# One core: attention into two feed-forward layers; attention products per head on 64 rows, a and b side by side in PSUM, the third weight group in one chunk

## The chip, the core and the metric

One core of a Trainium2 chip. The metric is the device time of one execution in microseconds; the kernel before takes 665.56 us (median of three runs). Matrix products run on TensorE (PE; its weight loads are listed as PEld), elementwise work on VectorE (DVE), ScalarE (ACT) and GpSimd (POOL); SyncE (SP) issues all transfers. Matmul results lie in PSUM: eight banks of 512 fp32 columns on 128 partitions.

## The reference

```python
kv = einsum('bhsd,bhse->bhde', k, v)              # 4 sequences, 8 heads, 576 tokens, head width 64
out = einsum('bhsd,bhde->bhse', q, kv)
x = out / sqrt(mean(out * out, -1) + 1e-6) * g_norm   # as 2304 tokens x 512
y = ((x @ w_a) * (x @ w_b)) @ w_out               # 512 -> 1536 -> 512, weights arrive as 64-bit floats
h = y @ w_in                                      # 512 -> 1024
solu = h * softmax(h)
out = layernorm(solu) * g_ln @ w_out2             # 1024 -> 512
```

## The kernel before, in words

All instructions are issued once, in an order that a planner in the kernel writes out: `Order` keeps a clock of its own, every PE item has a cost (`od.pe(cost, ...)`), and every chain of ACT, DVE, POOL and SP steps has due times from such costs. Each engine then runs its instructions in that order and waits only for data.

The 2304 tokens are 18 tiles of 128 (t = 0 to 17). A sequence has 576 tokens, so tiles 4 and 13 belong to two sequences. Two heads make a pair p, four pairs a token.

1. Attention, to about 64 us on PE. `att_kv` (lines 802 to 848) forms k^T v of each head (L822, and the last 64 tokens of a sequence at L830) and copies the two 64 x 64 blocks of a pair onto the diagonal of a 128 x 128 tile of `bds`, whose rest is zero (memset at L312). `att_1` (L850) multiplies q by it: for each pair one fp32 matmul with 128 rows and 128 columns (L868; four a tile, and eight with 64 weight columns in a tile of two sequences). An fp32 matmul stands in the trace as two records, each with its own weight load. A tile's result takes one PSUM bank, one of banks 6 and 7 by turns (`R_PA`), or half a place for tiles 2 and 3 (`EXTRA`). ACT squares it (L905) and copies it out (L907), DVE sums, POOL takes the root, DVE or POOL scales. Tiles 0 to 11 are turned on PE (`att_2`, L961) into ACT L971 and DVE L972; tiles 12 to 17 go through HBM (`att_hop`: `sx`, `yb`, ACT L937 and L941, DVE L942). Either way x ends as a high part `xh` and a low part `xl` in fp32r.

2. First layer, columns in 12 groups f of 128, tokens in six blocks j of 384. Every product of high and low parts is three matmuls (`three`, L978 to L980). For f = 0, 1 (`ab_items`) eight items a block give a = x w_a in one bank of a place (two adjacent banks) and b = x w_b in the other; then ACT copies a to SBUF (L1040), DVE multiplies b by it (L1041) and the product goes to HBM (`store_g`). These items fill PE between attention steps; a block needs its three tiles of x. f = 2, 3 (pair fp = 1) run as `plain_step`, the others (fp = 2 to 5) as `step_items`: a Strassen scheme with seven products per matrix (P1 to P7 in the order of `WSEQ`), for a and b (m = 0, 1) by turns, each accumulator in a bank of its own (`bank_take`), with sums on DVE (L1212, L1261, L1300) and copies on ACT (L1205, L1253, L1262, L1269) for each m apart. `x_sums` (L1056) makes the sums of x for it on DVE (L1078) and ACT (L1082) in banks 4 to 7.

3. Weights are decoded from 64-bit floats (L438 to L459), split into high and low, and stored to HBM in groups (`sums_w`, `to_hbm` through two staging tiles `stg`): for each pair fp and matrix m groups 0 (512 columns), 1 and 2 (sums, only where a Strassen step needs them), 4 and 3 (256 columns each). `w_fill` loads a group into a slot of `wt` when it is free; group 4 shares slot 2 with the weights of f = 1.

4. Then the second product of the first layer (L1382) and the second layer (L1524, the same lines 978 to 980 with `gw`). Nothing in them is changed.

Of the kernel before, what the change touches and what calls it, by code (L numbers as in the profile page):

```python
# [9 lines left out]
F32 = mybir.dt.float32  # L10
# [192 lines left out]
def attention_moe_moe_kernel(ctx: ExitStack, tc, kv_in, kv_tail, q_in, g_norm, w1, w_in, w_out2, g_ln, out):  # L203
# [62 lines left out]
    bds = [M(f"bd{i}", [P, NP, P], F32, M.R2 + 40960 + 2048 * i) for i in range(2)]  # L266
# [21 lines left out]
    a_t = [M(f"a{i}", [P, TB], F32, M.AB + 1536 * i) for i in range(4)]  # L288
    g_t = [M(f"g{i}", [P, TB], F32, (M.AB + 6144, M.AB + 7680, M.R2 + 43008)[i]) for i in range(3)]
    s_t = [[M(f"s{m}{i}", [P, TB], F32, M.R2 + 36864 + 3072 * m + 1536 * i) for i in range(2)] for m in range(2)]  # L290
# [20 lines left out]
    for t in bds:  # L311
        nc.vector.memset(t, 0.0)  # L312
# [94 lines left out]
    STG = Slots(2)  # L407
# [192 lines left out]
    def sums_w(k, f, su, sf, t):  # L600
# [3 lines left out]

        def have(t):
            if i == 0:
                w_pair[fp, m] = f, sf
            else:
                rest(t, *w_pair[fp, m], f, sf)

        def rest(t, w0, s0, w1_, s1):
            h = CH // 2
            extra, summed = has_group(fp, 4), has_group(fp, 1)
            users = {s0: 1 + summed, s1: 1 + extra + summed}
            rank = rank_of(k)
            first = [3]

            def used(s):
                def done(t):
                    users[s] -= 1  # L620
                    if not users[s]:
                        F.give(s)
                        decode_more()
                return done

            def group(g, src, then):
                n = WN[g]

                def fill(hi, lo):
                    return [("A", 0.1 + 0.5 * n / CH, lambda: nc.scalar.copy(out=hi, in_=src)),  # L630
                            ("X", (0.1 + 0.52 * n / CH, 0.2 + 1.12 * n / CH),
                             lambda e: tt(e)(out=lo, in0=src, in1=hi.bitcast(F32), op=ALU.subtract))]

                return lambda t: to_hbm((fp, m, g), n, fill, then, t, rank)
# [4 lines left out]
            def two_sums():  # L639
                a, b = ws_t  # L640

                def part(t):
# [9 lines left out]
                    (None, 0, used(s0)), (None, 0, used(s1)), (None, 0, part),  # L652
                    (None, 0, group(2, b, part)),
                ]

            group(0, w0, used(s0))(t)
            if extra:
                group(4, w1_[:, 0:h], used(s1))(t)

            group(3, w1_[:, h:], used(s1))(t)  # L660
            if not summed:
                return
# [1241 lines left out]
```

## Time and profile before

| | us |
|---|---|
| median of three runs (665.41 to 666.17) | 665.56 |
| the profiled execution | 662.99 |
| its span, first to last instruction | 661.1 |
| PE busy in the span | 647.4 |
| DVE busy | 511.0 |
| ACT busy | 320.9 |
| POOL busy | 217.9 |

The profiled execution is 2.57 us shorter than the median; 1.9 us of it lie outside the span. Times inside rows are from one execution; start times count from the start of the span. "128*64 128x64" is a matmul with 128 rows and 64 columns of weights and 64 moving columns. A row "x16" in a timeline merges 16 instructions; its duration runs to the end of the last one, so the start of the next row tells more of the pace.

### The profile page before, as it was taken

What the parts mean: (1) busy time and instruction counts of PE and PEld (TensorE: products, weight loads), DVE (VectorE), ACT (ScalarE), POOL (GpSimd) and SP (SyncE); (2) the same over time, 40 slices, a digit from 0 to 9 for tenths busy, and PEclk for the clock granted to TensorE, in tenths of its full rate; (3) what the DMA queues carried; (4) which work ended last, traced back from release to release, by engine and by line L of the source; (5) the groups of instructions that cost most, each with busy time, mean ns of one, the idle gap of its engine ahead of it and who ended that gap; (6) DMA issues with size and microseconds to landing.
All of it is one profiled execution on the core that took longest, in us unless ns stands there. A gap on an engine that the chain in (4) does not pass through costs nothing.

```text
span 661.1 us, 10563 instructions
## 1 busy us (share of the span) xinstructions
PE 647.4 (98%) x3674; PEld 594.7 (90%) x3674; DVE 511.0 (77%) x828; ACT 320.9 (49%) x577; POOL 217.9 (33%) x247
## 2 busy tenths in 40 slices
PE   5999999999999999999999999999999999999998
PEld 4899989999999999999999888888888888888887
DVE  2988799988889888998579868786389996677730
ACT  3866552434444434444335445453576665464431
POOL 1777220324221102001023314121677774452100
PEclk9999999999999999999999999999999999999999
DMA  8994787667588796899995644774705464533451
GB/s 329 390 325 159 249 267 256 231 240 285 187 324 313 266 382 251 313 396 373 329 358 164 191 129 128 235 242 154 274 1 175 143 187 148 155 108 105 128 175 49
DMA packets 94486, 150.66 MB, mean 228 GB/s; under 512 B 9568, under 2 KB 61536, under 8 KB 94432
## 3 DMA queue, kind: packets, MB, share of 16 engines
q1 hardware_dynamic: 94432, 149.98, 66.0%
q8 instruction: 29, 0.48, 0.3%
q14 instruction: 25, 0.20, 0.1%
HBM read 93.33 MB, written 56.62 MB: 227 GB/s over the span
## 4 chain that ended last, share of the span: by engine, by line
PE 91%; DMA 3%; DVE 3%; SPq 1%; ACT 1%; issue 1%; POOL 1%; DVEq 0%; ACTq 0%
PE ps L1382 21%; PE ps L979 18%; PE ps L980 18%; PE ps L978 18%; PE ps L1524 13%; PE ps L868 2%; DMA raw<-in_w 1%; DMA kv<-in_kv 1%; DMA yb<-sx 1%; DVE gl L1356 1%; PE ps L961 1%; PE ps L822 1%; SPq L934 1%; POOL r L898 1%; DVE u L455 0%
## 5 line engine op out<-in xcount | busy, mean ns | idle before, releaser
L1382 PE MATMUL ps<-gh,wo 128*128 128x512 f32 (+1 forms) x480 | 137.6, 367 | 0.0
L978 PE MATMUL ps<-xh,wt 128*128 128x384 f32 x384 | 129.6, 338 | 1.0 <-ACT xh L941 1.0
L979 PE MATMUL ps<-xl,wt 128*128 128x384 f32 x384 | 128.4, 334 | 0.3 <-DVE xl L942 0.3
L980 PE MATMUL ps<-xh,wt 128*128 128x384 f32 x384 | 128.3, 334 | 0.0
L1382 PEld LDWEIGHTS ps<-gh,wo 128*128 128x128 f32 x480 | 88.7, 188 | 11.2
L1382 PE MATMUL ps<-gl,wo 128*128 128x512 f32 (+1 forms) x240 | 88.2, 368 | 0.7 <-DVE gl L1356 0.7
L1524 PE MATMUL ps<-bo,ao 128*128 128x512 f32 x378 | 87.3, 389 | 0.0
L1524 PEld LDWEIGHTS ps<-bo,ao 128*128 128x128 f32 x378 | 70.8, 188 | 14.8 <-ACT bt L1565 0.2
L1356 DVE TENSOR_TENSOR gl<-gi,gh 128x512 fp32r<-128x512 f32 (+1 forms) x60 | 48.0, 803 | 35.8 <-ACT gh L1355 35.4
L978 PEld LDWEIGHTS ps<-xh,wt 128*128 128x128 f32 x384 | 72.1, 188 | 1.5 <-ACT xh L941 1.3
L979 PEld LDWEIGHTS ps<-xl,wt 128*128 128x128 f32 x384 | 72.1, 188 | 0.5 <-DVE xl L942 0.5
L980 PEld LDWEIGHTS ps<-xh,wt 128*128 128x128 f32 x384 | 72.1, 188 | 0.0
L1355 ACT CAST gh<-gi 128x512 fp32r<-128x512 f32 (+1 forms) x60 | 34.7, 580 | 76.9 <-PE ps L1382 62.7
L979 PE MATMUL ps<-gw,dh 128*128 128x512 f32 (+1 forms) x152 | 57.4, 378 | 0.0
L980 PE MATMUL ps<-gw,dl 128*128 128x512 f32 (+1 forms) x152 | 57.4, 378 | 0.0
L978 PE MATMUL ps<-gw,dh 128*128 128x512 f32 (+1 forms) x152 | 57.4, 378 | 0.0
L1382 PEld LDWEIGHTS ps<-gl,wo 128*128 128x128 f32 x240 | 45.0, 188 | 6.7 <-DVE gl L1356 1.0
L978 PE MATMUL ps<-th,wt 128*128 128x384 f32 x144 | 48.1, 334 | 0.0
L979 PE MATMUL ps<-tl,wt 128*128 128x384 f32 x144 | 48.1, 334 | 0.0
L980 PE MATMUL ps<-th,wt 128*128 128x384 f32 x144 | 48.1, 334 | 0.0
L438 ACT ACTIVATE u<-raw 128x512 f32<-128x512 f32 x52 | 34.7, 671 | 22.2 <-DMA raw<-in_w 6.4
L450 DVE SCALAR_TENSOR_TENSOR f<-raw,u 128x512 uint32<-128x512 uint32 x52 | 38.8, 745 | 0.4
(136 smaller groups left out, 1214.4 us busy)
## 6 DMA issues: line engine op xcount, KB each, us to landing
raw<-in_w SPq DMA_DIRECT2D x36, 512.0 KB, 5.9
gm<-g SPq DMA_DIRECT2D x72, 192.0 KB, 3.9
hb<-stg SPq DMA_DIRECT2D x26, 512.0 KB, 3.2
wt<-hb SPq DMA_DIRECT2D x26, 512.0 KB, 6.3
gi<-gm SPq DMA_DIRECT2D x36, 256.0 KB, 2.7
su<-ya SPq DMA_DIRECT2D x34, 256.0 KB, 2.5
kv<-in_kv SPq DMA_DIRECT2D x16, 512.0 KB, 7.3
ya<-su SPq DMA_DIRECT2D x32, 256.0 KB, 3.0
```

The costliest lines, as they stand in the source:

```text
L438: nc.scalar.activation(out=u, in_=w[:, :, 1].bitcast(F32), func=AF.Abs)
L450: nc.vector.scalar_tensor_tensor(out=fb, in0=w[:, :, 1], scalar=0xC0000000, in1=ub, op0=ALU.bitwise_and, op1=ALU.bitwise_or)
L822: nc.tensor.matmul(at(p)[h * D:(h + 1) * D], lhsT=k, rhs=v, start=c == 0 and p - pairs[0] < 2, stop=False, skip_group_check=True)
L868: nc.tensor.matmul(ps[m * w:(m + 1) * w, p * P:(p + 1) * P], lhsT=src[:, m * w:(m + 1) * w], rhs=bds[b % 2][:, p], start=True, stop=True)
L898: ("G", 1.76, lambda: nc.gpsimd.tensor_tensor(out=r, in0=r, in1=mhalf[:, 0:H], op=ALU.pow)),
L978: nc.tensor.matmul(o, lhsT=ah, rhs=bh, start=first, stop=False, skip_group_check=skip)
L979: nc.tensor.matmul(o, lhsT=ah, rhs=bl, start=False, stop=False, skip_group_check=skip)
L980: nc.tensor.matmul(o, lhsT=al, rhs=bh, start=False, stop=last, skip_group_check=skip)
L1355: ("A", 0.08 + 0.5 * k, lambda g=g, gh=gh: nc.scalar.copy(out=gh, in_=g)),
L1356: ("S", 0.08 + 0.54 * k, lambda g=g, gh=gh, gl=gl: nc.vector.tensor_tensor(out=gl, in0=g, in1=gh.bitcast(F32), op=ALU.subtract)),
L1382: nc.tensor.matmul(o, lhsT=x, rhs=y, start=f == 0 and n == 0, stop=f == NF1 - 1 and n == 2)
L1524: nc.tensor.matmul(o, lhsT=x, rhs=y, start=first and k == m == 0, stop=k == 1 and m == 2, skip_group_check=not first)
```

## The change

- `bds` holds 64 columns per pair instead of 128: head 0 on partitions 0 to 63, head 1 on 64 to 127. No zeros, no memset.
- `att_1` runs a matmul per head, on 64 rows: eight per tile (weights 64 rows x 128 columns, 64 moving columns), 16 of 64 x 64 in tiles 4 and 13. Head 0 writes one bank, head 1 the next, so a tile takes two banks: 6 and 7 together, or a place if enough are free (`two_banks`, `spare`). `att_2` and single `att_kv` steps take one bank of 6 and 7, or a place. The planner's cost of `att_1` falls from 0.9 (1.2) to 0.5.
- a and b of every block stand in the two banks of a place. In Strassen steps one ACT copy and one DVE sum then serve both m (768 columns instead of 384), the sum V goes to a place of its own, and all blocks end in one function, `product`, which keeps a in the tile that receives the product; the tiles `a_t` go.
- For fp = 1 group 4 has 512 columns and there is no group 3; group 0 is stored as soon as its own chunk is decoded; there is a third staging tile.
- `x_sums` waits until four groups of fp = 1 are in HBM, and ranks behind that pair's decoding.

```diff
-    bds = [M(f"bd{i}", [P, NP, P], F32, M.R2 + 40960 + 2048 * i) for i in range(2)]
+    bds = [M(f"bd{i}", [P, NP, D], F32, M.R2 + 40960 + 1024 * i) for i in range(2)]
...
-    stg = [[M(f"stg{i}{n}", [P, 2, n], F32R, M.STG + 4096 * i) for n in (CH, CH // 2)] for i in range(2)]
+    stg = [[M(f"stg{i}{n}", [P, 2, n], F32R, (M.STG, M.STG + 4096, M.AB)[i]) for n in (CH, CH // 2)]
+           for i in range(3)]
...
-    for t in bds:
-        nc.vector.memset(t, 0.0)
...
+        return plain > 0 if g == 4 else plain < NTB // 2 if g in (1, 2, 3) else True
+
+    def size_of(fp, g):
+        return CH if g == 4 and not has_group(fp, 1) else WN[g]
...
+    own = {6: 0.0, 7: 0.0}
+
+    def spare():
+        return sum(place_time(i) <= od.now for i in range(3)) >= 1 + (od.now > 27)
...
+    def two_banks():
+        if max(own.values()) <= od.now:
+            own[6] = own[7] = INF
+            return PS[:, 6:8], own_done(6, 7)
+        i, ps = ps_tile()
+        return ps, ps_done(i)
...
+    def two_ok():
+        return max(own.values()) <= od.now or spare()
+
+    def one_ok():
+        return min(own.values()) <= od.now or spare()
...
-            if not (R_X.ok() and R_SQ.ok() and R_R.ok()) or INF in ready:
+            if not (R_X.ok() and R_SQ.ok() and R_R.ok() and two_ok()) or INF in ready:
...
-            od.pe(0.9 + 0.3 * (len(seqs(i)) == 2), lambda: att_1(i))
+            od.pe(0.5, lambda: att_1(i))
...
             for m, b in enumerate(bs):
-                nc.tensor.matmul(ps[m * w:(m + 1) * w, p * P:(p + 1) * P], lhsT=src[:, m * w:(m + 1) * w],
-                                 rhs=bds[b % 2][:, p], start=True, stop=True)
+                for h in range(2):
+                    hs = slice(h * D, (h + 1) * D)
+                    nc.tensor.matmul(ps[m * w:(m + 1) * w, h, p * D:(p + 1) * D], lhsT=src[hs, m * w:(m + 1) * w],
+                                     rhs=bds[b % 2][hs, p], start=True, stop=True)
...
+    def product(f, j, slot, ps, t):
+
+        od.chain([(None, 0, when_ok((G_S,), lambda sg: [
+            ("A", AC, lambda: nc.scalar.copy(out=g_t[sg], in_=ps[:, 0, 0:TB])),
+            ("V", VT, lambda: nc.vector.tensor_tensor(out=g_t[sg], in0=ps[:, 1, 0:TB], in1=g_t[sg], op=ALU.mult)),
+            ps_done(slot), store_g(f, j, sg)]))], t=t)
...
-        if not sum_q or att_left[0]:
+        if not sum_q or att_left[0] or sum(k[0] == 1 for k in w_in_hbm) < 4:
...
-        rank = 4.5
+        rank = 5.075
...
-            parts = [[(0, 0), (0, 1)], [(4, 0), (3, 0)]][i]
+            parts = [[(0, 0), (0, 1)], [(4, 0), (3, 0) if mixed else (4, 1)]][i]
...
+            if name == "P1":
+                od.chain([("A", 2 * AC - 0.1, lambda: nc.scalar.copy(out=s1, in_=pair_of(X[1]))), is_("s1")], t=w)
...
+            def add(o, a, b):
+                return ("V", 2 * VT - 0.15, lambda: nc.vector.tensor_tensor(out=o, in0=a, in1=b, op=ALU.add))
+
+            if once("u0", ("P6", "made"), "s1"):
+                y = pair_of(Y[1])
+                od.chain([add(y, y, s1), ("A", 2 * AC - 0.1, lambda: nc.scalar.copy(out=s1, in_=y)),
+                          (None, 0, lambda w: (st.__setitem__("u2", w), sums_of(w)))], t=w)
+            if once("v0", ("P7", "made"), "s5"):
+                def go(w):
+                    if ps_ready() > w:
+                        od.chain([(None, 0, go)], t=w + 0.1)
+                        return
+                    place = ps_tile()
...
+                    od.chain([add(pair_of(place[1]), pair_of(Y[1]), s5), (None, 0, done)], t=w)
...
+        NEEDS = {"P2": "s1", "P7": "u2", "P3": "s5", "P4": "v"}
```

## Rows read from the trace of the kernel before

**Rows 1.** The page's first part: busy us of each engine, share, instructions.
```profile
PE 647.4 (98%) x3674; PEld 594.7 (90%) x3674; DVE 511.0 (77%) x828; ACT 320.9 (49%) x577; POOL 217.9 (33%) x247
```

**Rows 2.** Stretches: busy us (instructions) of PE, PEld, DVE, ACT, POOL; clock, DMA.
```profile
80.00:100.00 20.00, 18.71 (x106) 18.13 (x105) 15.92 (x26) 9.47 (x18) 4.62 (x4) 1.00 0.83 268
...
150.00:320.00 170.00, 170.00 (x983) 170.00 (x982) 147.42 (x284) 76.03 (x155) 28.42 (x30) 1.00 0.85 309
...
600.00:661.00 61.00, 57.91 (x279) 48.74 (x277) 29.11 (x37) 23.31 (x32) 7.04 (x16) 1.00 0.34 108
```

**Rows 3.** What PE waited for: us in total, times, longest.
```profile
PE ps L822 <- DMA kv<-in_kv: 7.3, 3, 4.1
...
PE ps L1382 <- DVE gl L1356: 0.7, 1, 0.7
```

**Rows 4.** Timeline of tiles 16 and 17: start, duration, instruction, count, wait before it.
```profile
60.33 1.05 PE L868 MATMUL ps<-bd,q 128*128 128x128 f32 x8
...
62.07 0.58 ACT L907 COPY x<-ps 128x512 f32<-128x512 f32 x1
...
63.30 1.05 PE L868 MATMUL ps<-bd,q 128*128 128x128 f32 x8
...
86.17 0.45 PE L978 MATMUL ps<-xh,wt 128*128 128x384 f32 x1 [1.01 <-ACT xh L941]
```

**Rows 5.** Timeline of PE in attention, same columns.
```profile
19.37 1.15 PE L822 MATMUL ps<-kv 128*64 128x64 f32 x32
20.45 0.34 PE L830 MATMUL ps<-tail 64*64 64x64 f32 x8
...
29.73 1.05 PE L868 MATMUL ps<-bd,q 128*128 128x128 f32 x8
30.54 0.42 PE L978 MATMUL ps<-xh,wt 128*128 128x384 f32 x1
...
35.62 2.08 PE L822 MATMUL ps<-kv 128*64 128x64 f32 x64
37.63 0.46 PE L830 MATMUL ps<-tail 64*64 64x64 f32 x16
...
45.02 1.95 PE L868 MATMUL ps<-bd,q 128*128 128x128 f32 x16
46.73 0.42 PE L978 MATMUL ps<-xh,wt 128*128 128x384 f32 x1
...
55.07 0.34 PE L980 MATMUL ps<-xh,wt 128*128 128x384 f32 x1
55.34 1.09 PE L868 MATMUL ps<-bd,qs 128*64 128x128 f32 x16
56.36 0.44 PE L978 MATMUL ps<-xh,wt 128*128 128x384 f32 x1
```

**Rows 6.** Weight loads of three lines: ns min/median/max, first and last start, shape.
```profile
L868 PEld LDWEIGHTS ps<-bd,q x128: 186/192/333, 13.9 to 64.0; 128*128 128x128 f32 x128
...
L822 PEld LDWEIGHTS ps<-kv x256: 132/138/232, 4.1 to 51.6; 128*64 128x64 f32 x128
...
L830 PEld LDWEIGHTS ps<-tail x64: 129/134/228, 5.2 to 52.0; 64*64 64x64 f32 x64
```

**Rows 7.** Groups by line and form: busy us, mean ns, idle before and its releaser.
```profile
L1078 DVE TENSOR_TENSOR ps<-ps,xl 128x768 f32<-128x768 f32 x15 | 14.4, 957 | 0.1
L1261 DVE TENSOR_TENSOR ps<-ps,s 128x384 f32<-128x384 f32 x24 | 13.5, 563 | 8.1 <-PE ps L980 4.5 <-ACT stg L578 2.2 <-ACT stg L630 1.4
...
L1253 ACT COPY s<-ps 128x384 f32<-128x384 f32 x24 | 11.5, 481 | 23.5 <-PE ps L980 19.1 <-issue 2.7 <-DVE u L455 1.6
...
L1082 ACT CAST th<-ps 128x768 fp32r<-128x768 f32 x9 | 7.2, 803 | 10.6 <-DVE ps L1078 10.5
```

**Rows 8.** The page's transfers: count, KB each, median us from issue to landing.
```profile
gm<-g SPq DMA_DIRECT2D x72, 192.0 KB, 3.9
...
wt<-hb SPq DMA_DIRECT2D x26, 512.0 KB, 6.3
```

More of the change, by code (lines that the diff above doesn't have):

```diff
@@ L603, in sums_w, with used, done, group @@
         fp, i = x // 2, x % 2
+        extra, summed = has_group(fp, 4), has_group(fp, 1)
+        rank = rank_of(k)
+        h = CH // 2
+        def used(s, n):
+            left = [n]
+            def done(t):
+                left[0] -= 1
+                if not left[0]:
+                    F.give(s)
+                    decode_more()
+            return done
+        def group(g, src, then):
+            n = size_of(fp, g)
+            def fill(hi, lo):
+                return [("A", 0.1 + 0.5 * n / CH, lambda: nc.scalar.copy(out=hi, in_=src)),
+                        ("X", (0.1 + 0.52 * n / CH, 0.2 + 1.12 * n / CH),
+                         lambda e: tt(e)(out=lo, in0=src, in1=hi.bitcast(F32), op=ALU.subtract))]
+            return lambda t: to_hbm((fp, m, g), n, fill, then, t, rank)
@@ L605, in have @@
         def have(t):
             if i == 0:
[L607 to L615, printed above, removed]
-            first = [3]
[L618 to L634, printed above, removed]
+                free0 = used(sf, 1 + summed)
@@ L791, in run_front @@
         else:
-            od.pe(0.9 + 0.3 * (len(seqs(i)) == 2), lambda: att_1(i))
+            od.pe(0.5, lambda: att_1(i))
     def back_ok():
-        return back and (R_PA.ok() or back[0][1] <= 3 and ps_ready() <= od.now)
+        return back and one_ok()
     def run_back():
@@ L805, in att_kv @@
         if n == 1:
-            sp = R_PA.take()
-            ps = PS[:, 6 + sp % 2:7 + sp % 2]
-            free = (None, 0, lambda t: R_PA.give(sp))
+            ps, free = one_bank()
+            ps = ps.unsqueeze(1)
         else:
@@ L952, in att_2 @@
     def att_2(t, x, sx):
[L953 to L958 removed]
+        ps, free = one_bank()
         xf = x.rearrange("t h d -> t (h d)")
@@ L1305, in step_items, with pair_of, block, ready @@
-        left = {(m, g): (2, 2, 2, 1)[g] for m in range(2) for g in range(4)}
-        steps_left[fp, t] = 14
-        return [item(m, *p) for p in WSEQ for m in range(2)]
-    s_free = [0.0] * 4
+        st = {}
+        steps_left[fp, t] = 14
+        left = {(m, g): (2, 2, 2, 1)[g] for m in range(2) for g in range(4)}
+        def pair_of(x):
+            return x[:, :, 0:TB]
+        def block(i, place, w):
+            product(2 * fp + (i > 1), 2 * t + i % 2, *place, w)
+        def ready(m, name, g, n):
+            w = max([w_at.get((fp, m, g), INF)] + ([x_sum.get((t, n), INF)] if n in (T1, T2, T3, T4) else []))
+            if m == 0 and name in ("P1", "P6", "P5"):
+                w = max(w, ps_ready())
+                if name == "P1":
+                    w = max(w, s_free[0])
+                elif name == "P5":
+                    w = max(w, s_free[1])
+            elif name in NEEDS:
+                w = max(w, st.get(NEEDS[name], INF))
+            elif name not in st:
+                w = INF
+            return w
@@ new lines, in run @@
+        def run(m, name, g, c, n):
+            at = {"P2": "P1", "P7": "P6", "P4": "P6", "P3": "P5"}.get(name, name)
+            first = at == name
+            if m == 0 and first:
+                st[name] = ps_tile()
+                if name != "P6":
+                    s_free[name == "P5"] = INF
+            slot, ps = st[at]
+            x = x_of(t, n)
+            for k in range(2):
+                sl = slice(c * 256 + k * P, c * 256 + (k + 1) * P)
+                w = wt[m][g]
+                three(ps[:, m, 0:TB], w[:, 0, sl], w[:, 1, sl], x[2 * k], x[2 * k + 1], first and k == 0, k == 1, not first)
+            left[m, g] -= 1
+            if not left[m, g] and t == NTB // 2 - 1:
+                slot_free[m, g] = od.now
+            steps_left[fp, t] -= 1
+            if m:
+                od.chain([(None, 0, lambda w: whole_one(name, w))], t=od.now + PC + 0.2)
@@ L1310, in attention_moe_moe_kernel @@
+        NEEDS = {"P2": "s1", "P7": "u2", "P3": "s5", "P4": "v"}
+        return [(PC, lambda m=m, p=p: ready(m, p[0], p[1], p[3]), lambda m=m, p=p: run(m, *p)) for p in WSEQ for m in range(2)]
+    s_free = [0.0] * 2
     steps_left = {}
```

254 lines of the change are left out of this document (79 added, 175 removed).

## The prediction, made before any run of the change

> **What bounds the kernel now.** First the page's busy times: PE works 647.4 of 661.1 us, DVE 511.0, ACT 320.9 [rows 1]. "Busy" alone does not show that PE is dense, so the second view is the busy time in stretches: from 150 to 320 us, the Strassen steps, PE has no idle time and 983 matmuls in 170 us, 173 ns each, while DVE is busy for 147 us and ACT for 76 [rows 2]. There a shorter ACT or DVE step buys nothing, and a later one costs something only when PE reaches it. The third view is what PE waited for: 7.3 us for the first k and v and 0.7 us for a split of the product [rows 3]; the only other wait of size is at 86.17, where the last block of x is not ready [rows 4], 1.3 us of idle time in the stretch 80 to 100 [rows 2]. The last 3.1 us of idle time lie in the tail after 600, which the change does not touch [rows 2]. So the time is the start, plus PE's work, plus about 2 us of stalls. A gain must come from PE's work in attention or from those 2 us.
>
> **The attention products: PE's work.** Today a tile of one sequence is four matmuls of 128 x 128 x 128, eight records: it starts at 29.73 and the next work at 30.54, two tiles from 45.02 to 46.73, so eight more records take 0.90 us, 112 ns each [rows 5]. After it is eight matmuls, 16 records, of 64 rows x 128 columns with 64 moving columns, half on the lower and half on the upper 64 rows. That the two row halves run beside each other is seen in the tail of k and v: 64 x 64 matmuls on two row halves and two column halves take 0.46 us for 16 records and 0.34 for eight, 15 ns a record, four at a time in 60 ns [rows 5]. So a tile has 8 slots with two records each; the question is the slot.
>
> No row has 128 columns loaded and 64 moved. The bound from below is the nearest row with 64 moved: k^T v, two column halves at a time, goes from 1.08 us for 32 records to 2.01 for 64, 58 ns a slot [rows 5]. The bound from above is the nearest with 128 loaded, today's 112 ns. Which end rules is told by the weight loads: 192 ns for 128 columns, 138 for 64 columns on 128 rows, 134 for 64 columns on 64 rows [rows 6]. Fewer rows save nothing; 64 columns more cost 54 to 58 ns, so 128 columns have about 110 ns of work in them, and the slot of 112 is the load's own length. Each record brings its own load, also in the new form. I take 112: eight slots, 0.90 us, as today. The shorter moving side then hides behind the load and saves nothing.
>
> What it costs is the change of shape. Before the two-sequence tile the next start comes 0.27 us after the last instead of 0.173, 0.10 more, when 128*128 gives way to 128*64 (55.07 to 55.34); its 16 records then hold PE for 1.02 us, 0.12 more than eight slots of 112 [rows 5]. Going back I take the same 0.10, so 0.20 a run of tiles, with 0.33 as the upper bound (both excesses and once more the first). On PE the tiles after the first four stand in these runs: 5 and 6 together, 7, 8, 9, 10 and 11 together, 14, 15, 16, 17: nine runs, 1.8 us. Tile 12 stands directly before k^T v, whose shape differs anyhow: 0.1. Tiles 0 to 3 stand between two such and cost nothing new. The two-sequence tiles get 32 records of 64 x 64, four at a time in 60 ns: 0.48 instead of 0.90, twice, -0.85, and their change of shape exists already. Sum: 1.8 + 0.1 - 0.85 = +1.0 us of PE work; with 0.33 a run it is +2.3.
>
> **The planner's cost and the stall at 86.** The planner now counts 0.5 for a tile, where it counted 0.9 and 1.2, and fills what it believes free with dense blocks. Eleven tiles run once dense work has begun: ten times 0.4 and once 0.7, 4.7 us more dense work ahead of tile 17. That tile's way to PE takes from 63.30 to 86.17, 22.9 us [rows 4], through SP's queue. Cover: of the three blocks that stand behind the wait today one (f = 1, j = 4) needs nothing of tile 17; it has 24 matmuls of 0.173, 4.2 us, and the planner can move it ahead. So 4.7 against 4.2, and I keep the stall as it is. Without that cover the stall would grow by up to 4.7 us. The two memsets of the start lie beside the first loads, for which PE waits up to 4.1 us at a time [rows 3]: nothing.
>
> **a and b side by side.** In a Strassen step six ACT copies of 481 ns become three of about 803, two block copies become four; six DVE sums of about 0.56 us become three of 957 ns (prices from the forms with 768 columns) [rows 7]. DVE saves 0.5 us and ACT adds 0.5 per step, both beside PE [rows 2]: zero. Deadlines are now for both m together. An item is six matmuls, 1.04 us. Between P6 and P7 stand four items, 4.2 us, for a sum and a copy of 1.8; between P1 and P2 two, 2.1 us, for a copy of 0.8; between P7 and P4 two, 2.1 us, for a sum of 0.96 that may first wait for another DVE instruction of up to 0.96. All are met. The fourth place, taken by V, must be free for the next P1 4.2 us after P7: sum 0.96, copy 0.48, product 0.56, 2.0 us. A `g` tile is now taken from the copy on, 0.6 us earlier, and is held 3.9 us by its store [rows 8]: four blocks a step, 20 us of the 43.8 that three tiles give in 14.6 us. If these margins fail, one late sum can cost up to 1 us in each of 12 steps.
>
> **Third group and x sums.** Six stores and loads per pair of matrices become four, of equal bytes. Group 4 with 512 columns needs slot 2, which the last plain block of f = 1 frees; its load lands 6.3 us later [rows 8], and two blocks of group 0, 8.3 us, come first: hidden by 2.0, and if that goes it costs the difference once. The x sums start later, but behind 50 us of plain steps; DVE has 0.96 us for each of them [rows 7]: zero. On SP two issues fewer stand ahead of the return of tile 17; in between -0.9 and 0, taken as 0.
>
> **Sum.** Profiled execution 662.99 + 1.0 = 664.0. The median lies 2.57 above the profiled one: 666.6 us.
>
> **Rivals.**
> *The load hides after all.* If the slot is 58 ns, 16 tiles save 8 x 54 ns each, 6.9 us, against 1.0 of the above: PE has 5.9 us less. For: moved columns are halved, and nothing shows this shape. Against: loads scale with columns [rows 6]. If tile 17 moves forward with PE, all of it counts: 659.7; if its transfers hold it, PE waits longer at 86 and nothing is left: 665.6. Middle 662.5.
> That is also what a rule gives: the Trainium skill, "TensorEngine Tiling (Array Packing)", section "Theoretical Speedup", states up to twice the throughput for a contraction of 64 or less. By it the time would be this rival's; the trace agrees for 64 x 64 matmuls and no run shows it for 128 weight columns.
>
> *Slower: banks run out in attention.* A tile now takes two banks, 6 and 7, from its first matmul to the end of its copy, 60.33 to 62.65, 2.3 us [rows 4]; today it takes one of them. After 27 us a place is lent only if two of three are free, and a dense block in work holds one, its product often the next. If never lent, 41 to 64 us holds nine tiles of 2.3 us, 20.7 us, plus four turns of about 2 us (on one bank, partly side by side), 4 to 8: 25 to 29 us of 22. Tile 17 comes 3 to 7 us later, and the cover of 4.2 us at the stall is spent already. From half of this on, at least 1.5 to 3.5 us, it decides the time: about 669, at worst 671.
> The same skill page, section "Gotcha 1: PSUM Pressure", warns that row tiles need different banks; the change obeys it, and that is where the second bank comes from.
>
> *Strassen margins fail:* half a microsecond in 12 steps, 672.6. Against: PE has nothing but work there [rows 2], and the margins above.
>
> *The stall at 86 goes* because the planner finishes attention sooner: 666.6 - 1.3 - 0.5 = 664.8.
>
> **Chances.** Forecast (load-bound, stall as it is, 665.6 to 668) 0.35; load hidden 0.28; banks 0.20; stall gone 0.10; Strassen 0.07. 0.2% of the time, 1.3 us, is about what a measurement of this kernel can tell from no change. Below 664.2 fall most of "load hidden" (0.25) and half of "stall gone" (0.05): faster 0.30. Between: the lower part of the forecast (0.25), half of "stall gone" and the rest of "load hidden": 0.33. Above 666.9: 0.10 of the forecast, banks and Strassen: 0.37. The range takes in all but the far ends of "load hidden" and "banks" and the Strassen case: 661 to 670.5; the forecast's own range is 665.6 to 668.
>
> **What would show it.** Right: a one-sequence tile of L868 still holds PE for about 0.9 us, with gaps near 0.1 at both ends, and its loads still last about 190 ns; two-sequence tiles hold it near 0.5. Wrong: 16 records in about 0.5 us. For the banks: PE waits for ACT's L907 in attention or idles longer than 1.3 us near 86 to 92. For the margins: PE idle time between 150 and 320. It would be wrong altogether if the start moved: first-layer matmuls that begin well before or after their place of today, just ahead of 29.73 [rows 5].

## The result, and the profile after

The changed kernel takes 670.76 us (median; 670.23 to 671.33) against 665.87 for the kernel before in the same comparison: 1.0073 times as long, 95% interval 1.0056 to 1.0090. The profiled execution takes 670.23 us, its span is 668.1; before it was 662.99 and 661.1. So the two profiles lie 7.0 us apart in span, the medians 4.9. Both numbers need an explanation, and the last experiment gives the one for their difference.

Lines have moved: attention products L868 are now L895, k^T v L822 is L852 (tail L860), turns L961 are L984, `three` is L1001 to L1003, the x sums L1078 are L1098.

The page's first part after, for [rows 1]:

```profile
PE 653.9 (98%) x3834; PEld 597.9 (89%) x3834; DVE 503.5 (75%) x784; ACT 326.5 (49%) x563; POOL 225.4 (34%) x251
```

PE has 6.5 us more work. The stretches, same columns as [rows 2]:

```profile
80.00:100.00 20.00, 20.00 (x118) 20.00 (x117) 17.17 (x35) 9.64 (x17) 0.00 (x0) 1.00 0.75 246
100.00:120.00 20.00, 18.48 (x105) 17.90 (x105) 18.10 (x27) 7.70 (x14) 6.20 (x6) 1.00 0.83 285
150.00:320.00 170.00, 168.93 (x973) 168.10 (x972) 144.83 (x252) 80.10 (x140) 38.28 (x37) 1.00 0.87 320
```

The idle time at 86 is gone; there is new idle time between 100 and 120 (1.5 us) and between 150 and 320 (1.1 us). What PE waited for, columns as in [rows 3], names it:

```profile
PE ps L852 <- DMA kv<-in_kv: 7.3, 3, 4.1
PE ps L1001 <- DMA wt<-hb: 1.5, 1, 1.5
PE ps L1001 <- ACT s L1230: 0.9, 1, 0.9
...
PE ps L895 <- DMA q<-in_q: 0.3, 1, 0.3
PE ps L984 <- DVE x L927: 0.3, 1, 0.3
PE ps L1001 <- ACT s L1253: 0.2, 1, 0.2
```

The timeline of PE, for [rows 4] and [rows 5]; first the start, then one tile among first-layer products:

```profile
13.83 7.68 PE L895 MATMUL ps<-bd,q 64*128 64x64 f32 x64
21.44 1.97 PE L852 MATMUL ps<-kv 128*64 128x64 f32 x32
...
27.36 0.69 PE L895 MATMUL ps<-bd,qs 64*64 64x64 f32 x32
...
30.36 0.42 PE L1001 MATMUL ps<-xh,wt 128*128 128x384 f32 x1
...
62.24 0.34 PE L1003 MATMUL ps<-xh,wt 128*128 128x384 f32 x1
62.51 1.11 PE L895 MATMUL ps<-bd,q 64*128 64x64 f32 x16
63.55 0.45 PE L1001 MATMUL ps<-xh,wt 128*128 128x384 f32 x1
63.83 0.34 PE L1002 MATMUL ps<-xl,wt 128*128 128x384 f32 x1
```

And the loads of L895, the answer to [rows 6] (ns min/median/max):

```profile
L895 PEld LDWEIGHTS ps<-bd,q x256: 182/188/335, 13.8 to 72.2; 64*128 64x128 f32 x128
L895 PEld LDWEIGHTS ps<-bd,qs x64: 129/135/135, 27.4 to 59.0; 64*64 64x64 f32 x64
```

The start is the surprise. The same 32 records of k^T v that took 1.15 us before [rows 5] take 1.97, nearly twice as long: TensorE still runs at 1.2 GHz there, where before it ran at 2.4. The trace's list of the granted clock says the same: its first entry, at full clock, is at 17.5 us before and at 26.2 after (ahead of a first entry the view of stretches prints 1.00, so there the pace of equal instructions is the better witness).

Where the difference builds up is seen when the starts of the n-th first-layer matmul (two profiles of one kernel, same n) are set side by side. The third column is a later profile of the kernel before, explained with the last experiment:

| first-layer matmul | before | before, third profile | after | after minus before |
|---|---|---|---|---|
| 1st | 28.59 | 28.73 | 30.36 | +1.8 |
| 145th, behind attention | 72.52 | 72.64 | 78.32 | +5.8 |
| 253rd, behind the stall at 86 | 93.08 | 96.43 | 97.04 | +4.0 |
| 361st, behind the gap near 114 | 111.80 | 115.15 | 117.79 | +6.0 |
| 685th, behind the first Strassen step | 167.96 | 171.32 | 175.57 | +7.6 |
| end of PE's last instruction | 657.9 | 661.2 | 664.9 | +7.0 |

So against the profile of before: attention +5.8, the stall at 86 -1.8, a new stall near 114 +2.0, the first Strassen step +1.6, later -0.6. Inside attention, PE's time from each start to the next, waits apart, grew by 4.0 us for tiles of one sequence (2.1 of it in the first four), 1.5 for k^T v, 0.7 for the turns and 0.9 for first-layer products next to a tile; two-sequence tiles gave back 1.15, waits 0.2.

The chain of work that ended last, from a decoded chunk to the gap near 114, and at the first Strassen step (start us, us, what):

```profile
101.79 0.70 DVE stg L623
102.50 8.67 DMA hb<-stg
111.23 4.27 DMA wt<-hb
115.63 0.41 PE ps L1001
...
166.07 0.19 PE ps L1003
166.29 0.81 ACT s L1230
167.14 0.45 PE ps L1001
```

### The profile page after: what moved, and what is told of

Read it like the earlier page. It is cut to its first block, busy times and chain, and to the rows that moved or that the text cites. A ratio compares the mean times of both kernels' runs of the same rounds, so it can differ in the third digit from the quotient of the medians.

```text
span 668.1 us, 10827 instructions
## 1 busy us (share of the span) xinstructions
PE 653.9 (98%) x3834; PEld 597.9 (89%) x3834; DVE 503.5 (75%) x784; ACT 326.5 (49%) x563; POOL 225.4 (34%) x251
## 4 chain that ended last, share of the span: by engine, by line
PE 94%; DMA 4%; ACT 1%; DVE 1%; SPq 0%; issue 0%; ACTq 0%; DVEq 0%
PE ps L1353 22%; PE ps L1001 18%; PE ps L1002 18%; PE ps L1003 18%; PE ps L1495 13%; PE ps L895 3%; DMA hb<-stg 1%; PE ps L852 1%; DMA kv<-in_kv 1%; DMA q<-in_q 1%; DMA wt<-hb 1%; PE ps L984 1%; PE ps L860 0%; SPq L381 0%; ACT bd L866 0%
## 5 line engine op out<-in xcount | busy, mean ns | idle before, releaser
L1001 PE MATMUL ps<-xh,wt 128*128 128x384 f32 x384 | 129.9, 338 | 2.4 <-DMA wt<-hb 1.5
L1003 PE MATMUL ps<-xh,wt 128*128 128x384 f32 x384 | 128.4, 334 | 0.0
L1001 PEld LDWEIGHTS ps<-xh,wt 128*128 128x128 f32 x384 | 72.1, 188 | 3.8 <-DVE tl L1098 1.8
L1327 DVE TENSOR_TENSOR gl<-gi,gh 128x512 fp32r<-128x512 f32 (+1 forms) x60 | 45.6, 767 | 37.3 <-ACT gh L1326 37.2
L1003 PEld LDWEIGHTS ps<-xh,wt 128*128 128x128 f32 x384 | 72.1, 188 | 0.0
L1003 PE MATMUL ps<-gw,dl 128*128 128x512 f32 (+1 forms) x152 | 57.4, 378 | 0.0
L1001 PE MATMUL ps<-gw,dh 128*128 128x512 f32 (+1 forms) x152 | 57.4, 378 | 0.0
L1040 DVE TENSOR_TENSOR g<-ps,g 128x384 f32<-128x384 f32 x72 | 39.4, 553 | 21.3 <-ACT g L1039 8.4
L1039 ACT COPY g<-ps 128x384 f32<-128x384 f32 x72 | 34.0, 482 | 41.8 <-DVE ps L1249 19.5
L1001 PE MATMUL ps<-th,wt 128*128 128x384 f32 x144 | 48.3, 335 | 0.2 <-ACT s L1253 0.2
L1003 PE MATMUL ps<-th,wt 128*128 128x384 f32 x144 | 48.1, 334 | 0.0
```

The lines of the kernel that those rows point to most:

```text
L1001: nc.tensor.matmul(o, lhsT=ah, rhs=bh, start=first, stop=False, skip_group_check=skip)
L1003: nc.tensor.matmul(o, lhsT=al, rhs=bh, start=False, stop=last, skip_group_check=skip)
L1039: ("A", AC, lambda: nc.scalar.copy(out=g_t[sg], in_=ps[:, 0, 0:TB])),
L1040: ("V", VT, lambda: nc.vector.tensor_tensor(out=g_t[sg], in0=ps[:, 1, 0:TB], in1=g_t[sg], op=ALU.mult)),
L1327: ("S", 0.08 + 0.54 * k, lambda g=g, gh=gh, gl=gl: nc.vector.tensor_tensor(out=gl, in0=g, in1=gh.bitcast(F32), op=ALU.subtract)),
```

## Experiments

Ratios are to the kernel before on the same chip. "Whole rows" means one matmul a pair on 128 rows, with the zeros of `bds` back.

**The first four tiles on 128 rows.**

```diff
+    def whole_rows(t):
+        return t < 4
...
+                if whole_rows(t):
+                    nc.tensor.matmul(ps[m * w:(m + 1) * w, 0, p * P:(p + 1) * P], lhsT=src[:, m * w:(m + 1) * w],
+                                     rhs=bds[b % 2][:, p], start=True, stop=True)
+                    continue
```

> The changed kernel with one thing undone: tiles 0 to 3 (the first sequence) are multiplied on 128 rows again, all later tiles per head on 64 rows; places, planner and the rest as changed. Theory (the clock): in the kernel before TensorE's granted clock rose from 1.2 to 2.4 GHz at 17.5 us, while the first four tiles ran; in the changed one only at 26.2, after the 64-row products of these tiles had ended and k and v of the second sequence had run on 128 rows. If the 64-row products hold it back, the clock now rises near 17.5 us, the four tiles take 5.5 us instead of 7.6, the 32 records of k and v behind them 1.15 instead of 1.97, the first layer begins near 28.6 instead of 30.4, and the time falls by 3 to 4 us to about 667.3. Rival (the rise came late by itself, and the form of these tiles has no part in it): k and v still take near 2.0 us, the time stays within 0.7 us of 670.8.

Measured: 1.0099 (1.0074 to 1.0123). In the profile the clock rises at 17.9 us:

```profile
19.99 1.15 PE L854 MATMUL ps<-kv 128*64 128x64 f32 x32
...
26.38 0.66 PE L995 MATMUL ps<-ident,x 128*128 128x128 f32 x4 [1.02 <-DVE x L938]
...
29.05 0.66 PE L995 MATMUL ps<-ident,x 128*128 128x128 f32 x4 [0.97 <-DVE x L938]
29.46 0.42 PE L1012 MATMUL ps<-xh,wt 128*128 128x384 f32 x1
```

The theory is right on the clock and wrong on the time: k^T v is back at 1.15 us, but PE now waits 2.0 us for x, and the 145th first-layer matmul starts at 78.14, 0.2 earlier than in the changed kernel.

**The whole attention part undone.** Whole rows in all tiles; the rest as changed.

```diff
-        ps, free = two_banks()
+        ps, free = one_bank()
...
-            od.pe(0.5, lambda: att_1(i))
+            od.pe(0.9 + 0.3 * (len(seqs(i)) == 2), lambda: att_1(i))
```

> The changed kernel with its whole attention part undone: all tiles on 128 rows into one bank, planner's cost 0.9 and 1.2 again; a and b side by side, the third group and the x sums as changed. Theory (attention costs 5.8 us by the end of tile 17, and gives 1.8 back at the stall near 86; the late group 4 costs 1.65 us, the first Strassen step 1.6, a stall of 0.9 near 367 is gone): the early stall returns, the later two remain, 667.5 to 668.5, with idle time of PE near 110 and near 160. Rival (all of the loss is attention, the later stalls follow from it): about 665, with no stall near 110 or 160.

Measured: 1.0010 (0.9993 to 1.0028): the rival, nearly. Nearly all of the loss in the median depends on the attention part. The gap near 110 is gone with it, so the late group 4 is a consequence. The wait in the first Strassen step stays (0.9 us for the copy s, 1.3 in all by the starts of the matmuls), so that one isn't:

```profile
PE ps L1010 <- ACT s L1239: 0.9, 1, 0.9
```

**The x sums as before, and the third group as before.**

```diff
-        if not sum_q or att_left[0] or sum(k[0] == 1 for k in w_in_hbm) < 4:
+        if not sum_q or att_left[0]:
...
-        rank = 5.075
+        rank = 4.5
```

> The changed kernel with the x sums as before: no waiting for four stored groups, rank 4.5 again. Theory (the x sums, 9 us later at their end than before, hold four banks into the first Strassen step, which needs whole places): the sums end near 163, the gaps of 0.35 and 1.05 us at 161 and 166 and the small ones beside them go, 1.6 us less, about 669.2. Rival (a place is short in that step whenever the sums end, or the copies are late for another reason): the gaps stay, 670.8. Third outcome: the sums delay the decoding of the weights and the stall near 114 grows beyond 1.65 us.

Measured: 1.0097 (1.0075 to 1.0118). The first sum starts 6 us earlier (96.65 instead of 102.73), the last still ends late, and the wait of 0.9 us in the first step stays (1.3 in all). The rival holds, and the step belongs to a and b side by side: from the 361st to the 685th first-layer matmul all 13 profiles with them side by side take 57.5 us or more, whenever the sums begin, and all seven of versions of the kernel before 56.2. Why it does is argued, not shown: the sums hold four of eight banks until their end, and the step needs a third place. No run separates that.

```diff
-        return plain > 0 if g == 4 else plain < NTB // 2 if g in (1, 2, 3) else True
+        return plain > 0 if g == 4 else plain < NTB // 2 if g in (1, 2) else True
...
+                group(4, f[:, 0:h], free1)(t)
+            group(3, f[:, h:], free1)(t)
```

> The changed kernel with the third group undone: for fp = 1 groups 4 and 3 of 256 columns each again, the x sums wait for all six groups. Theory (the load of 512 columns into slot 2 can't start before its whole chunk is decoded and stored, and lands too late: store 8.7 us, load 4.3): the gap of 1.65 us near 114 goes, about 669.1. Rival (the transfers are crowded then, with a busy share of 0.95 to 0.98 from 95 to 110, and the same bytes land no earlier in two pieces): the gap stays between 1.2 and 2.2 us, 670.8.

Measured: 1.0088 (1.0065 to 1.0111), with a gap of 1.06 us ahead of 105.93 in place of the one near 114. Two chunks don't cure it; mostly the rival.

**The planner's cost alone, and the form alone.**

```diff
-            od.pe(0.5, lambda: att_1(i))
+            od.pe(1.1 - 0.5 * (len(seqs(i)) == 2), lambda: att_1(i))
```

> The changed kernel with one number different: the planner counts 1.1 us for a tile of one sequence and 0.6 for one of two, instead of 0.5, which is nearer to what the tiles hold PE for (1.25 alone, 1.07 in a pair, 0.8 with two sequences). Only the order of the work changes. Theory (the loss is the form of the products: the late clock and 0.355 us at the two ends of each run of tiles): PE's work is the same, so 0 to 1 us less than the changed kernel, 669.5 to 670.8. Rival (the planner's low cost puts dense blocks and transposes in a wrong order, and that is most of the 5 us): 666 to 667.5.

And the converse, the cost left at 0.5 and whole rows for every tile:

```diff
+    def whole_rows(t):
+        return True
```

> The changed kernel with only the form of the products undone: all tiles on 128 rows, a matmul per pair; each tile still takes two banks, the planner's cost is still 0.5. Theory (form): the clock rises near 17.5, each later run of tiles costs 0.36 us less and the two tiles of two sequences 0.4 more each, so most of the loss goes: 665 to 666.5. Rival (two banks a tile and the cost of 0.5 hold attention back, as in the run with only the first four tiles on 128 rows, where PE waited for x instead): 668 to 670.

Measured: cost alone 1.0039 (1.0017 to 1.0060), form alone 1.0008 (0.9987 to 1.0029). Both give back a part that the other theory did not allow. With the right cost the wait for group 4 near 114 is gone; only 99 first-layer matmuls instead of 111 stand ahead of the last tile (96 before). With whole rows the cost of 0.5 and the two banks do no harm in the median. In the profile they do: 111 matmuls stand ahead of the last tile, and PE waits for x at the start and for group 4 at 112.6:

```profile
PE ps L995 <- DVE x L938: 1.7, 2, 1.1
PE ps L1012 <- DMA wt<-hb: 1.7, 1, 1.7
```

The table behind the last experiment shows why the median hides this.

**Extra products while PE waits for loads**, of a constant 128 x 128 tile with itself, in the changed kernel and in the one before:

```diff
+        for _ in range((5, 4, 2, 1)[pairs[0]] if b == 0 else 0):
+            nc.tensor.matmul(PS[:, 5, 0:P], lhsT=warm, rhs=warm, start=True, stop=True)
```

> The changed kernel with idle time of TensorE filled: ahead of the four steps of k and v of the first sequence 5, 4, 2 and 1 extra fp32 products of a constant 128 x 128 tile with itself, into a bank that nobody reads then; they run while PE waits for the loads. Nothing else is changed. Theory (the clock is held at 1.2 GHz by what PE does early, and full 128 x 128 products let it rise): it rises before 12 us, the first four tiles take about 3.6 us instead of 7.6. PE then waits for x as in the run with the first four tiles on 128 rows, so the time falls by 0.5 to 3 us only: 668 to 670. Rival (the clock needs the later work to rise): 670.8, and the four tiles take 7.6 us still.

> The kernel before with the same extra products ahead of the first four steps of k and v. Theory: the clock rises before 12 us instead of at 17.5, the first four tiles take 3.6 us instead of 5.5 and the first layer begins 1 to 2 us earlier, if x is ready then; the time falls by 0.5 to 2 us against the kernel before. Rival (x of tiles 0 to 2 sets the start of the first layer): the time is that of before within 0.5 us.

Measured: 1.0047 (1.0025 to 1.0069) and 0.9959 (0.9944 to 0.9974). In the profile of the changed kernel the clock rose at 27.0 us all the same, in spite of 12 us of nearly gapless work ahead of the tiles:

```profile
0.00:14.00 14.00, 12.09 (x104) 10.24 (x104) 3.52 (x7) 3.81 (x9) 0.72 (x7) 1.00 0.88 308
```

In the kernel before it rose at 6.9, and fell again at 20.55, while PE waited 2.33 us for x of tile 0 (timeline, then the stretch, where the number behind the five engines is the granted clock):

```profile
21.59 1.08 PE L965 MATMUL ps<-ident,x 128*128 128x128 f32 x4 [2.33 <-DVE r L897]
22.61 1.98 PE L826 MATMUL ps<-kv 128*64 128x64 f32 x32
```

```profile
20.40:27.40 7.00, 5.81 (x62) 4.94 (x64) 5.66 (x9) 3.60 (x10) 6.63 (x5) 0.51 1.02 365
```

So with the same extra products one clock had risen ahead of the first tile and the other had not; what decides that stays open. Four of the ten executions of the changed one have a mean granted clock of 0.990 to 0.992, which the profiled one (1.000) has not, so its course differs between executions.

The second version is the only one whose interval lies below both kernels. Its profile, of 664.28 us, is the slowest of its seven executions, and PE waits only 0.3 us for x near 86 in it, against 1.3 to 2.9 us in the three of the kernel before. What that is worth is told behind the last experiment.

**Both undone at the start and in the planner; two attempts at a faster version.** First the changed kernel itself, unedited, for the comparison on one chip:

> The changed kernel itself once more, on the chip of the three runs beside it. So far it was 1.0073 of the kernel before, and versions of it with 64-row products in all tiles were at 1.0039 (planner's cost 1.1) to 1.0097 (x sums early). Theory: the form of the products and the planner's cost together make the loss, 1.006 to 1.010 here, with the clock rising between 25 and 27 us in the profiled run as in the five runs with 64-row first tiles so far. Rival: the 0.4% between the planner's costs was a difference of chips; then 1.003 to 1.005.

Then the edit of the first experiment and the cost together:

```diff
+    def whole_rows(t):
+        return t < 4
...
+            od.pe(1.1 - 0.5 * (len(seqs(i)) == 2), lambda: att_1(i))
```

> The changed kernel with tiles 0 to 3 on 128 rows and the planner's cost at 1.1 and 0.6; later tiles per head on 64 rows. Each alone gave -0.2 us at the end of attention and 1.0039 of the time of before. Theory (the early clock could not count alone, since PE then waited 2.6 us for x of the first tiles, which the low cost lets it reach too soon): with both, those waits go, the first layer begins before 29.3 us, and the time is 1.000 to 1.003 of the kernel before. Rival (the two edges of each run of 64-row tiles, eight times 0.36 us, are enough by themselves): 1.0035 to 1.005.

Then the kernel before with two-sequence tiles (4 and 13) per head, each into both banks of a place and counted at 0.75 instead of 1.2, and more extra products, eight of them ahead of the first turn:

```diff
-    EXTRA = (2, 3)
+    EXTRA = (2, 3, 4, 13)
...
-            od.pe(0.9 + 0.3 * (len(seqs(i)) == 2), lambda: att_1(i))
+            od.pe(0.9 - 0.15 * (len(seqs(i)) == 2), lambda: att_1(i))
...
+        for _ in range((6, 5, 5, 3)[pairs[0]] if b == 0 else 0):
+            nc.tensor.matmul(PS[:, 5, 0:P], lhsT=warm, rhs=warm, start=True, stop=True)
...
+        for _ in range(8 if t == 0 else 0):
+            nc.tensor.matmul(ps[:, 0:P], lhsT=warm, rhs=warm, start=True, stop=True)
```

> The kernel before with two things added: the tiles of two sequences (4 and 13) per head on 64 rows into the two banks of a place, and extra products of a constant 128 x 128 tile while PE waits at the start, 6, 5, 5 and 3 ahead of the first four steps of k and v and 8 ahead of the first turn of x. The extra products alone, in smaller number, gave 0.9959. Theory: the two tiles save 0.4 us of PE each and the clock does not fall again at 20.5 us: 0.992 to 0.996, below both kernels. Rival (x of tile 0 sets the start, extra products delay it): 0.998 to 1.002.

And the changed one with the same products:

```diff
+    def whole_rows(t):
+        return len(seqs(t)) == 1
...
+            od.pe(0.9 - 0.15 * (len(seqs(i)) == 2), lambda: att_1(i))
```

> The changed kernel with tiles of one sequence on 128 rows in one bank, the two tiles of two sequences per head in two banks, the planner's cost 0.9 and 0.75, and the same extra products; a and b side by side, third group and x sums as changed. With all tiles on 128 rows it was at 1.001. Theory: 0.993 to 0.998; it beats the kernel before by the early clock and the two tiles, as the version built on the kernel before does. Rival (the stall in the first Strassen step, 1.3 us, and the late group 4 eat it): 0.998 to 1.002.

Measured: changed kernel 1.0077 (1.0054 to 1.0099); first four tiles and cost 1.0006 (0.9990 to 1.0022); the attempts 1.0025 (1.0006 to 1.0044) and 1.0011 (0.9992 to 1.0029). So the first four tiles and the cost together bring the median back, while 14 tiles stay in the new form; the edges of the runs are not enough for the loss. The profile of the first attempt loses at another place: PE waited 2.0 us for the transfer of a weight group near 100, and the clock fell for 3.4 us behind it.

**Which tiles' cost, and the first four tiles per head in the kernel before.**

```diff
+    def whole_rows(t):
+        return t < 4
...
+            od.pe(0.9 if i < 4 else 0.5, lambda: att_1(i))
```

> The changed kernel with tiles 0 to 3 on 128 rows and counted at 0.9 by the planner; later tiles per head on 64 rows and counted at 0.5 as changed. Theory A (the start: the early clock counts as soon as the planner's order at the start fits): the waits for x ahead of the first layer (2.6 us with the cost of 0.5) go, the first layer begins before 29 us, and about half of the loss is back: 1.003 to 1.005 of the kernel before. Theory B (what the cost does, it does in the later tiles: more dense work ahead of the last tile, the late decoding of group 4): the time stays at 1.006 to 1.010.

```diff
+            od.pe(0.5 if i < 4 else 1.1 - 0.5 * (len(seqs(i)) == 2), lambda: att_1(i))
```

> The changed kernel with the cost of tiles 0 to 3 left at 0.5 and that of the later tiles at 1.1 (0.6 with two sequences); all tiles per head on 64 rows. With 1.1 for all tiles it was 1.0039 of the kernel before. Theory A (the cost matters at the start): 1.006 to 1.008, as the changed kernel. Theory B (it matters in the later tiles): 1.003 to 1.005, and the wait of 1.7 to 2.2 us for group 4 near 114 is gone, as there.

```diff
-    EXTRA = (2, 3)
+    EXTRA = (0, 1, 2, 3)
```

> The kernel before with only tiles 0 to 3 per head on 64 rows, each in both banks of a place (banks 0 to 5 for these four tiles, so the fourth waits for the first one's copy); all else as before, planner's cost too. Theory (the 64-row products of the first four tiles hold the clock at 1.2 GHz): it rises between 25 and 27 us in the profiled run instead of at 17.5, k and v behind the four tiles take 1.97 us for 32 records instead of 1.15, the first layer begins 2 to 4 us later and the time is 1.003 to 1.006 of the kernel before. Rival (the clock's late rise comes with the rest of the change): it rises near 18, and the time is within 0.2%.

Measured: 1.0101 (1.0071 to 1.0132), 1.0052 (1.0032 to 1.0072), 0.9990 (0.9969 to 1.0011). The cost does its harm in the later tiles: theory B twice, though both times lie 0.0001 to 0.0002 above its ranges. Its way differs. In the first kernel no wait for group 4 is left, but PE waits 1.9 us for a sum on DVE in the first Strassen step; and in five of its six executions the mean granted clock is 0.997 or less, for a reason that its profile, the sixth, can't show. In the third kernel the clock is late again (26.7), and the first layer starts 2.6 us later, which costs nothing in the median:

```profile
14.00 7.09 PE L873 MATMUL ps<-bd,q 64*128 64x64 f32 x64
21.02 1.97 PE L822 MATMUL ps<-kv 128*64 128x64 f32 x32
...
31.18 0.42 PE L988 MATMUL ps<-xh,wt 128*128 128x384 f32 x1
```

**The kernel before, profiled twice more, and the last version once more**, all three unedited.

> The kernel before itself, profiled a second time. Its profiled execution took 662.99 us, 2.6 below the median of its other runs, and the kernel with only the first four tiles per head was 4.2 us longer in its profiled execution but equal in the median. Theory (the single profiled execution of before is an early-clock, short-stall one; in others the clock rises later): here the clock rises after 20 us, or the span is 663 us and more. Rival (the clock always rises near 17.5 us with 128-row first tiles, and the spread comes from later stalls, that near 86 above all): rise at 16 to 19 us, with other stalls than in the first profile.

> The kernel before, profiled a third time: same question as in the second profile. Theory: the rise of the clock differs between the executions by several us. Rival: 16 to 19 us each time, and the span moves by 1 to 3 us through stalls behind 80 us.

> The kernel before with only tiles 0 to 3 per head on 64 rows, profiled a second time. Theory (the 64-row products hold the clock): rise at 25 to 27 us again, first layer 2 to 3 us later than in the profiles of the kernel before, and a span 2 to 3 us above the mean of its three. Rival: a rise near 18 us, or a late rise with a span like that of before, so that the late start is made up behind attention.

Measured: 0.9991 (0.9955 to 1.0027), 0.9997 (0.9970 to 1.0024) and 0.9976 (0.9953 to 1.0000), with profiled executions of 667.53, 666.19 and 664.28 us. The clock's rise is early in both of before (15.0, which is 1 us below the rival's range, and 18.2) and late in the last (25.6). So the theory of a late clock in the kernel before falls, though both spans are above 663 us, as it allowed too, and the three rises differ by 3.2 us. The rivals hold best, the last one's too: its span of 662.5 is like those of before. What differs is the stall near 86. In the first profile PE waited 1.0 us there [rows 4]; in the second one this (wait, then stretches with the clock behind the five engines):

```profile
PE ps L978 <- ACT xh L941: 2.6, 1, 2.6
```

```profile
84.00:86.50 2.50, 0.73 (x5) 0.41 (x3) 1.41 (x4) 1.04 (x2) 0.00 (x0) 1.00 0.99 169
86.50:90.00 3.50, 2.67 (x7) 2.27 (x8) 3.16 (x6) 1.63 (x4) 1.29 (x1) 0.53 0.81 265
90.00:93.50 3.50, 3.50 (x12) 3.50 (x12) 2.66 (x4) 1.97 (x4) 1.30 (x2) 0.50 0.84 256
93.50:100.00 6.50, 6.50 (x40) 6.50 (x38) 5.06 (x8) 1.65 (x4) 0.00 (x0) 1.00 0.78 250
```

Within the wait of 2.6 us the clock falls to half, for 6.8 us (in the third profile 1.9 us behind the wait, for 3.4), and from the 145th to the 253rd matmul these two profiles lose 4.1 and 3.2 us more than the first. In the version with the first four tiles per head, whose PE arrives there later, the wait is 0.4 us (1.3 in its first profile) and the clock stays up: its late start is made up at 86:

```profile
PE ps L988 <- ACT xh L951: 0.4, 1, 0.4
```

This is why 7.0 us between two profiles are 4.9 between medians: with the mean of the three profiled executions of before, 665.57, and the two of the changed kernel, 670.23 and 670.27, the difference is 4.7.

The executions without a profile bear it out, since each has its mean granted clock on record; a fall of 3.4 us or more makes it 0.997 or less (the late rise at the start is not counted in it). Of 125 executions of the kernel before beside these experiments, 57 had the clock up throughout and took 663.4 us in the mean, 68 lost some of it and took 666.1; where they lost it is on record for the profiled ones only. The changed kernel had it up in 9 of 10. So its loss against the kernel before is 6.6 us when the clock stays up in both, and 4.9 between medians because the kernel before so often loses 2.6. The same comparison, clock up on both sides and on the same chip (differences below about 1 us are not told apart by so few executions):

| version | executions with the clock up | us above the kernel before |
|---|---|---|
| changed kernel, again | 6 of 6 | 6.6 |
| first four tiles on 128 rows | 2 of 4 | 5.7 |
| planner's cost of 1.1 and 0.6 | 10 of 10 | 4.6 |
| whole rows, cost of 0.5, two banks | 9 of 10 | 2.8 |
| first four tiles and cost | 12 of 12 | 2.1 |
| whole attention part undone | 10 of 10 | 1.1 |
| kernel before, first four tiles per head (two runs) | 10 of 12, 8 of 8 | 0.4, 0.6 |

What is left with the attention part undone is about the 1.3 us of the first Strassen step; the low cost and two banks under whole rows do cost something, some 1.7 us more (2.8 against 1.1, on two chips). And the 0.9959 of the kernel before with extra products goes with a mean of 663.2 us, no less than the 663.1 of the 12 of 28 executions of the kernel before on that chip that kept the clock up: it avoids most of the stall at 86, and no version here is shown to beat the kernel before when that keeps the clock.

## Why the prediction was wrong, point by point

The sum for the profiled execution was 664.0; it is 670.23. The range ended at 670.5, the median is 670.76.

*The slot: right.* Fewer rows save nothing: 188 ns a load on 64 rows with 128 columns, and the pairs of L895 start 112 ns apart (837 ns from the first to the last of 16 records). The rival "load hidden" is refuted. The Trainium skill, "TensorEngine Tiling (Array Packing)", section "Theoretical Speedup", allows up to twice the throughput; of that upper limit nothing is reached here, where 128 columns are loaded for 64 that move. Two-sequence tiles take 0.48 us from the first to the last record, as forecast.

*The change of shape: mechanism right, term mis-sized.* The step said 0.20 a run, with 0.33 as the bound. One tile among first-layer products costs 0.89 us before and 1.25 after, a pair 1.79 and 2.14: 0.355 a run. Ahead of the run 0.10 is lost, as taken; behind it the exit takes 0.20 instead of 0.03, which no row of before showed. The Trainium skill, "TensorEngine Tiling (Array Packing)", section "Key Properties", says that a change of tiling mode drains the array; the trace agrees in so far as time is lost at both ends, 0.355 us a run. Without waits, the later tiles cost PE 1.9 us more and the first-layer products beside them 0.9, and the two-sequence tiles give back 1.15 instead of 0.85: +1.6 us net instead of +1.0.

*"Tiles 0 to 3 stand between two such and cost nothing new": this step failed.* They cost 2.1 us more and k^T v behind them 1.5, because the clock stays at 1.2 GHz until 25 to 27 us. All nine profiles with 64-row products in these tiles show it, and in all eight without extra products and with whole rows it rises between 15.0 and 18.8. The text had named a moved start as what would make it wrong altogether, but had no term for it. The shown price in time is smaller than these 3.6 us. Alone it is worth nothing in the median, because PE then meets the wait for x (changed kernel with the first four tiles on 128 rows) or escapes the stall at 86 (kernel before with them per head). With the right cost it is 0.33% (1.0039 against 1.0006, on one chip), some 2 us.

*The planner: "4.7 against 4.2, and I keep the stall" failed in the size of both.* 15 first-layer matmuls more stand ahead of the last tile, 2.6 us at 0.173, and block f = 1, j = 4 did move ahead of the wait as thought possible, so the stall went. It was also worth more than the one profile told: 1.0 us of waiting there, but 2.6 and a slow clock in two others. The price of the low cost came where the text saw none: attention ends 8.2 us later (tile 17 at 71.45 instead of 63.30), of which the 15 matmuls are 2.6, and the decoding of fp = 1 with it. The right cost gave back 0.2 to 0.4% (1.0073 and 1.0077 against 1.0052 and 1.0039).

*Third group: "lands 6.3 us later ..., hidden by 2.0" failed.* The load was counted from the freeing of its slot. What ended last was its data: the store was issued at 102.50, took 8.67 us with the DMA engines 0.95 to 0.98 busy, and the load 4.27. The text had "it costs the difference once", but only for another cause.

*Strassen margins and x sums: eleven steps as said, one not.* The idle time between 150 and 320 is 1.1 us, nearly all in the first step, where sums and products share PSUM. "Zero" was mis-sized by 1.6 us, 1.3 of it in every version with a and b side by side.

*The offset.* Adding 2.57 to pass from profile to median carried the luck of one execution of before, in which the clock did not fall at the stall, over to a kernel that has no stall at 86. After, the profiled execution lies 0.53 below the median.

*Banks run out:* the forecast time of this rival, 669 to 671, came true (670.76) by luck, without its mechanism. No wait of L895 for a copy out of PSUM stands among PE's waits; and two banks a tile with a cost of 1.1 left 99 or 69 first-layer matmuls ahead of the last tile (cost in all or only in the later tiles), against 96 before and 111 at 0.5, so it is the cost that sets the order. Its stretch of 41 to 64 us is 23 us, too, not 22.

## What to carry to other kernels

Before a product is cut into smaller tiles, find what its slot is made of: if it is the load, fewer rows and fewer moving columns gain nothing, and each change of shape costs. A planner's cost has to follow what an instruction group holds its engine for, ends included; 0.5 for 1.25 us did a third to half of the damage here. And a single profile of a kernel with a wait of 1 to 3 us on TensorE needs a second one, since the wait may or may not take the clock down with it.

## What was not expected of the hardware

- With 64-row fp32 products in the first four tiles TensorE stayed at 1.2 GHz for 7.6 us of unbroken work, in one profile even behind 12 us of nearly full work; in that of the changed kernel the clock rose behind them, while 128-row k^T v ran.
- Waits of 2.3 to 2.65 us went with 3.4 or 6.8 us at half clock (three profiles; in two of them it fell before the wait was over), waits of 1.5 and 2.2 us in the two profiles of the changed kernel did not; one of 2.0 us in another version did.
- A store of 512 KB took 8.67 us at a DMA share of 0.96, against a median of 5.0.
